# Attention scores: eight half-filled array tiles against four full ones with block-diagonal keys

## The chip, the cores and the metric

The kernel runs on one core of a Trainium2 chip. A core has TensorE (matrix products into PSUM), VectorE, ScalarE and GpSimd (elementwise work, named DVE, ACT and POOL in the profile), and SyncE (SP), whose queue issues most DMAs. The engines run their own instruction streams and meet at semaphores. The metric is the device time of one execution in microseconds; lower is better.

## The reference

The input x has 2048 rows of 512 values in bf16. Both branches read the same layer norm of it, and the output is x plus both branches.

```python
def _A_ref(x, wqkv, wo):
    H = 32; Dh = D // H; W = 256          # Dh = 16
    q, k, v = ...                          # of x @ wqkv, by heads
    scores = jnp.einsum("bhqd,bhkd->bhqk", q, k) * (Dh ** -0.5)
    mask = (idx[:, None] - idx[None, :] >= 0) & (idx[:, None] - idx[None, :] < W)
    p = _softmax(jnp.where(mask[None, None], scores, -1e9), axis=-1)
    o = jnp.einsum("bhqk,bhkd->bhqd", p, v)
    return (lambda x, *d: x.transpose(*d))(o, 0, 2, 1, 3).reshape(B, S, D) @ wo

def _B_ref(x, w_gate, w_up, w_down):       # F = 1792
    g = jnp.einsum("bsd,df->bsf", x, w_gate)
    u = jnp.einsum("bsd,df->bsf", x, w_up)
    return jnp.einsum("bsf,fd->bsd", g * u, w_down)

xn = _layernorm(x, axis=-1)
return x + _A_ref(xn, A_wqkv, A_wo) + _B_ref(xn, B_w_gate, B_w_up, B_w_down)
```

A has 32 heads of only 16 dimensions, and each query sees the 256 keys up to its own place.

## The kernel before

**Tiling.** The rows are cut into four chunks of 512 (T = 0 to 3). The 512 columns of Q and K are four groups (c = 0 to 3) of 128, which lie on the 128 partitions with the 512 rows of the chunk along the free dimension: `proj_qk` multiplies and copies one such tile from PSUM. Eight heads of 16 dimensions share a tile; every 32 partitions (a row group e of TensorE's array) hold an even head in the first 16 and an odd head in the last 16. Keys are taken in blocks of 64, queries in runs of 64 to 320.

**Scores.** `scores` makes one step: a batch of two or three pieces with 512 query columns in all. A piece is one block of 64 keys of one group c against a run of queries, for all eight heads. TensorE's array is used in tiles of 32 rows by 64 columns, so that eight small matmuls stand beside each other: four row groups e by two parities `par`. The even head (par 0) is multiplied with the plain K from the first 16 rows. The odd head (par 1) uses 32 rows of a second tile `Ko`, in which the even head's rows are zero. `Ko` is made by VectorE from `K` by a product with the per-partition scalar `odd` (0 or 1), at L262. The scores land in S, four PSUM banks of [128, 512], with the even head's 64 keys on partitions 0 to 63 and the odd head's on 64 to 127. S has one buffer. ScalarE then writes P = exp(S / 4) for all four banks at once (L319). GpSimd (`triangle`, L158) and VectorE (`mask_diag`, L343) zero what the window excludes.

**Values.** `values` (L366) multiplies P with V or VS (V with its halves swapped, by DMA), in 64x32 array tiles. There are two PSUM banks per (T, c), and mostly two groups are done in one burst, 192 matmuls. VectorE transposes the result (L372), and `divide` normalises it.

**The rest.** `proj_v`, `gate`, `up`, `down` and `wo` are plain 128x128 matmuls with 512 columns. All of them, and `proj_qk` and `values`, take their PSUM banks from one ring of four (`ps_m`).

**What sets the order.** The order on every engine is written out by a planner in `run`. There are 75 score steps (15 for T = 0, 20 for each later chunk). Between two steps, `fill` issues "fillers", mostly half a projection (two matmuls of 512 columns), until a target of TensorE time is reached; `SHIFT` moves this target at some steps. The planner counts in units of one such matmul. `book` keeps a count of when ScalarE and VectorE come free; `copy` gives each copy out of PSUM to the one that its booking says would be done first. The constants `EXP`, `MASK`, `HALF`, `COPY` and so on are the booked costs. They steer the choices and are no instructions themselves. In `first_chunk` the copies of K(0, 0) and K(0, 1) go to VectorE and that of Q(0, 0) to ScalarE; the first score step follows.

Of the kernel before, what the change touches and what calls it, by code (L numbers as in the profile page):

```python
# [7 lines left out]
BF16 = mybir.dt.bfloat16  # L8
F32 = mybir.dt.float32
# [16 lines left out]
GAP = 10.6  # L26
PAIRS = ((0,), (1,), (2,), (3,)), ((0, 1), (2, 3)), ((0, 1), (2, 3)), ((0, 1), (2,))
SHIFT = {20: -2, 21: -5, 22: -8, 23: -11, 24: -14, 26: -10, 27: -7, 28: -3, 62: 3, 63: 6, 64: 12, 66: 12, 67: 11, 68: 9, 69: 6, 70: 3}
MASKED, FIRST_DIVIDE, SECOND_DIVIDE = 8, 8, 24
COPY = dict(act=2.8, dve=3.2)  # L30
EXP, MASK, HALF, SUMS, DIVIDE, TURN, STATS = 8.7, 1.9, 1.7, 4.2, 8.2, 6.1, 4.2


class Kernel:
# [26 lines left out]
    def setup(self):  # L61
        nc, const, NT, NF = self.nc, self.const, self.NT, self.NF
        self.x = const.tile([128, NT, 512], BF16, name="x")
        self.Wqkv = const.tile([128, 4, 1536], BF16, name="Wqkv")
        self.Wo = const.tile([128, 4, 512], BF16, name="Wo")
        self.Wg = const.tile([128, 4, self.F], BF16, name="Wg")
        self.Wu = const.tile([128, 4, self.F], BF16, name="Wu")
        self.Wd = const.tile([128, NF, 512], BF16, name="Wd")
        xv = self.x_d.rearrange("(t p) d -> p t d", p=128)
        wq = self.w_d["qkv"].rearrange("(k p) n -> p k n", p=128)  # L70
        wg = self.w_d["g"].rearrange("(k p) n -> p k n", p=128)
        wu = self.w_d["u"].rearrange("(k p) n -> p k n", p=128)
        for lo, hi in ((0, 1), (1, 2), (2, 4)):
            nc.sync.dma_start(out=self.x[:, lo:hi, :], in_=xv[:, lo:hi, :])  # L74
        for lo in (1024, 512, 0):
            nc.sync.dma_start(out=self.Wqkv[:, :, lo:lo + 512], in_=wq[:, :, lo:lo + 512])
        h = self.F // 2
        for lo in (0, h):
            nc.sync.dma_start(out=self.Wg[:, :, lo:lo + h], in_=wg[:, :, lo:lo + h])
            nc.sync.dma_start(out=self.Wu[:, :, lo:lo + h], in_=wu[:, :, lo:lo + h])  # L80
            if lo == 0:
                nc.sync.dma_start(out=self.x[:, 4:8, :], in_=xv[:, 4:8, :])
        nc.sync.dma_start(out=self.Wd[:], in_=self.w_d["d"].rearrange("(f p) n -> p f n", p=128))
        wo = self.w_d["o"].rearrange("(c p) n -> p c n", p=128)
        for c in range(4):
            nc.sync.dma_start(out=self.Wo[:, c, :], in_=wo[:, c, :])
        for lo, hi in ((8, 10), (10, 12), (12, NT)):
            nc.sync.dma_start(out=self.x[:, lo:hi, :], in_=xv[:, lo:hi, :])

        warm = const.tile([128, 1], F32, name="warm")  # L90
        nc.vector.memset(warm[:], 0.0)
        nc.scalar.activation(out=warm[:], in_=warm[:], func=ACT.Exp)
        self.idle = const.tile([128, 128], BF16, name="idle")
        nc.vector.memset(self.idle[:], 0.0)
        self.keep_busy(40)
        ident = const.tile([128, 128], BF16, name="ident")
        nc.gpsimd.memset(ident[:], 0.0)
        nc.gpsimd.affine_select(out=ident[:], in_=ident[:], compare_op=ALU.not_equal, fill=1.0,
                                base=0, pattern=[[-1, 128]], channel_multiplier=1)
        self.ident = ident  # L100
        pi = const.tile([128, 1], I32, name="pi")
        nc.gpsimd.iota(pi[:], pattern=[[0, 1]], base=0, channel_multiplier=1)
        podd = const.tile([128, 1], I32, name="podd")
        nc.vector.tensor_scalar(out=podd[:], in0=pi[:], scalar1=4, scalar2=1,
                                op0=ALU.arith_shift_right, op1=ALU.bitwise_and)
        self.odd = const.tile([128, 1], F32, name="odd")
        nc.vector.tensor_copy(out=self.odd[:], in_=podd[:])
        self.mhalf = const.tile([128, 4], F32, name="mhalf")
        nc.gpsimd.memset(self.mhalf[:], -0.5)
        self.diag = const.tile([128, 64], BF16, name="diag")  # L110
        self.far = const.tile([128, 64], BF16, name="far")
        nc.gpsimd.memset(self.diag[:], BIG)
        nc.gpsimd.memset(self.far[:], BIG)
        for half in (slice(0, 64), slice(64, 128)):
            self.triangle(self.diag[half], True)
            self.triangle(self.far[half], False)
        self.xnT, self.Q, self.hT, self.OT = {}, {}, {}, {}
        self.K, self.Ko, self.V, self.VS = {}, {}, {}, {}
        self.strips, self.parts, self.at = {}, {}, {}
        self.stock = []  # L120
        self.new_values()
# [124 lines left out]
    def proj_qk(self, T, c, is_k, ks=range(4), engine=None):  # L246
        nc = self.nc
        lo = 512 * is_k + 128 * c
        ps = self.bank(ks, "qkp")
        for k in ks:  # L250
            nc.tensor.matmul(ps[:], lhsT=self.Wqkv[:, k, lo:lo + 128], rhs=self.xnT[T][:, :, k, :],  # L251
                             start=(k == 0), stop=(k == 3))
        if 3 not in ks:
            return
        if is_k:
            self.K[T, c] = self.kpool.tile([128, 512], BF16, tag="K", name="K")
            self.Ko[T, c] = self.kpool.tile([128, 512], BF16, tag="Ko", name="Ko")
        else:
            self.Q[T, c] = self.qpool.tile([128, 512], BF16, tag="Q", name="Q")
        self.copy((self.K if is_k else self.Q)[T, c][:], ps[:], engine)  # L260
        if is_k:
            nc.vector.tensor_scalar(out=self.Ko[T, c][:], in0=self.K[T, c][:],  # L262
                                    scalar1=self.odd[:, 0:1], scalar2=None, op0=ALU.mult)
            self.book("dve", HALF)

    def first_chunk(self):

# [32 lines left out]
    def scores(self, T, pieces):  # L300

        nc = self.nc
        S = self.s_tiles.tile([128, 4, 512], F32, tag="S", name="S")
        P = self.ppool.tile([128, 4, 512], BF16, tag="P", name="P")
        col = 0
        for c, m, q0, q1 in pieces:
            U, j = divmod(8 * T + m, 8)
            keys, q, n = slice(64 * j, 64 * j + 64), 64 * q0, 64 * (q1 - q0 + 1)
            for par in range(2):
                for e in range(4):  # L310
                    rows = slice(32 * e, 32 * e + 16 + 16 * par)
                    nc.tensor.matmul(S[64 * par:64 * par + 64, e, col:col + n],  # L312
                                     lhsT=(self.Ko if par else self.K)[U, c][rows, keys],
                                     rhs=self.Q[T, c][rows, q:q + n],
                                     start=True, stop=True, tile_position=(32 * e, 64 * par),
                                     skip_group_check=True)
            self.parts.setdefault((T, c), []).append((P, col, m, q, n))
            col += n
        nc.scalar.activation(out=P[:, :, 0:col], in_=S[:, :, 0:col], func=ACT.Exp, scale=0.25)  # L319
        self.book("act", EXP)  # L320
        self.masked = self.free["act"]
        self.strips[(T, pieces)] = P
        for at in self.places(pieces, 4):
            for half in (slice(0, 64), slice(64, 128)):
                self.triangle(P[half, :, at:at + 64], False)
# [199 lines left out]

    def run(self):
        self.xns, self.stats, self.sums = {}, {}, {}
        self.now, self.free = 0, dict(act=0, dve=0)
        self.setup()
        NCH = self.NCH  # L530
# [21 lines left out]
        def fill(upto, group):  # L552
            nonlocal spent, n
            while n < len(work):
                cost, f, before, after = work[n]
                if after is not None and after > valued:
                    break
                if spent + cost / 2 > upto and not any(
                        w[2] is not None and w[2] <= group for w in work[n:]):
                    break  # L560
                spent += cost
                self.now = spent
                f()
                n += 1
                while pending and spent >= pending[0][0]:
                    pending.pop(0)[1]()

# [5 lines left out]
        held = None  # L573
        for g, s in enumerate(steps):
            keys = due.get(g, [])
            if held is None:
                valued = ready
                fill(-1, g + len(keys) // 2)
# [87 lines left out]
```

The softmax here doesn't subtract the row's maximum and nothing guards it: scores larger than these inputs give would overflow.

## Time and profile before

| | before |
|---|---|
| median of 3 runs | 264.86 us (264.67 to 265.57) |
| profiled execution, its own time | 265.39 us |
| its span in the profile | 263.7 us |
| TensorE busy | 259.4 us (98%) |
| VectorE busy | 175.1 us (66%) |
| ScalarE busy | 175.5 us (67%) |
| GpSimd busy | 116.9 us (44%) |
| score matmuls (L312) | 1440 in 75 steps |
| `Ko` products (L262) | 16, mean 404 ns |
| granted TensorE clock | full over the whole span |

In the profile a line names a kernel line, an engine, an operation, and tiles as out<-in with their shapes; "x4" counts instructions, and the busy time and mean duration follow. A bracket such as [0.17 <-PE qkp L251] is the idle time before an instruction and what ended it. TensorE has two rows: PE for matmuls and PEld for the loads of their stationary operand. A list of waits has, on each line, who waited for whom, then the total in us, how many times, and the longest.

### The profile page before, as it was taken

To read this page: it belongs to the slowest core of one execution; us is meant where nothing else is said; L and a number is where in the kernel's file an instruction comes from. 1 tells how busy PE (TensorE), PEld (TensorE's weight loads), DVE (VectorE), ACT (ScalarE), POOL (GpSimd) and SP (SyncE) were. 2 spreads that over 40 slices of the span, in tenths; PEclk is the share of its full clock that TensorE was granted. 3 is DMA by queue.
4 is the path that set the end of the run, shared out by engine and by line. 5 is a ranking of instruction groups with operands and counts; after the bars stand their busy time and mean duration, and the time that the engine had idled before them with its cause. 6 is when DMAs were issued, how large, how long until landed. Compare 5 with 4: busy or idle time off the path is not lost.

```text
span 263.7 us, 8896 instructions
## 1 busy us (share of the span) xinstructions
PE 259.4 (98%) x3890; PEld 120.9 (46%) x3890; DVE 175.1 (66%) x342; ACT 175.5 (67%) x141; POOL 116.9 (44%) x278
## 2 busy tenths in 40 slices
PE   8999999999999999999999999999999999999996
PEld 8444444444444544444544454444544445444453
DVE  6677888877845497567873669766685135977344
ACT  3376788888856866677776566767777546787600
POOL 6216342425457645334456644544453451463600
PEclk9999999999999999999999999999999999999999
DMA  6999921220002600002001310000100100000002
GB/s 180 378 357 340 281 29 22 24 47 4 0 25 57 84 2 0 4 0 47 5 0 42 81 45 2 0 2 19 32 4 0 42 21 22 5 0 2 4 2 80
DMA packets 19431, 15.12 MB, mean 57 GB/s; under 512 B 7360, under 2 KB 19392, under 8 KB 19392
## 3 DMA queue, kind: packets, MB, share of 16 engines
q1 hardware_dynamic: 18848, 14.26, 19.9%
q8 instruction: 30, 0.49, 0.8%
q10 hardware_dynamic: 544, 0.30, 0.4%
q14 instruction: 9, 0.07, 0.1%
HBM read 9.70 MB, written 2.10 MB: 45 GB/s over the span
## 4 chain that ended last, share of the span: by engine, by line
PE 96%; DMA 2%; SPq 0%; issue 0%; DVE 0%
PE gp L395 19%; PE up L406 19%; PE psd L428 17%; PE qkp L251 11%; PE S L312 10%; PE acc L366 6%; PE vp L239 5%; PE psd L434 5%; PE L L428 2%; DMA Wqkv<-in_A_wqkv_dram 2%; PE L L434 1%; PE L L366 0%; SPq L74 0%; PE xTp L209 0%; DVE x L444 0%
## 5 line engine op out<-in xcount | busy, mean ns | idle before, releaser
L319 ACT ACTIVATE P<-S 128x2048 bf16<-128x2048 f32 x75 | 140.7, 1876 | 50.6 <-PE S L312 46.8
L158 POOL TENSOR_SCALAR_AFFINE_SELECT P<-P 64x256 bf16<-64x256 bf16 x224 | 100.9, 450 | 126.3 <-ACT P L319 112.1
L395 PE MATMUL gp<-xnT,Wg 128*128 128x512 bf16 x224 | 60.1, 380 | 0.0
L406 PE MATMUL up<-xnT,Wu 128*128 128x512 bf16 x224 | 59.1, 380 | 0.0
L411 DVE TENSOR_TENSOR hT<-up,gsb 128x512 bf16<-128x512 f32 x56 | 38.3, 685 | 19.3 <-PE up L406 13.7
L428 PE MATMUL psd<-Wd,hT 128*128 128x512 bf16 (+1 forms) x210 | 48.0, 369 | 0.0
L343 DVE TENSOR_TENSOR P<-P,diag 128x512 bf16<-128x512 bf16 (+1 forms) x75 | 29.4, 392 | 6.1 <-ACT P L319 6.1
L428 PEld LDWEIGHTS <-hT 128*128 128x128 bf16 x238 | 21.3, 98 | 25.1 <-issue 2.9
L406 PEld LDWEIGHTS <-Wu 128*128 128x128 bf16 x224 | 20.5, 98 | 25.4 <-issue 2.5
L395 PEld LDWEIGHTS <-Wg 128*128 128x128 bf16 x224 | 20.3, 98 | 25.1 <-issue 1.9
L312 PE MATMUL S<-Q,K 16*64 16x320 bf16 (+4 forms) x720 | 31.0, 260 | 0.0
L312 PE MATMUL S<-Q,Ko 32*64 32x320 bf16 (+4 forms) x720 | 30.9, 260 | 0.0
L251 PE MATMUL qkp<-xnT,Wqkv 128*128 128x512 bf16 x128 | 29.9, 380 | 0.0
L230 ACT ACTIVATE gsb<-gp 128x512 bf16<-128x512 f32 x39 | 22.9, 596 | 8.2 <-PE gp L395 7.4
L312 PEld LDWEIGHTS <-K 16*64 16x64 bf16 x720 | 12.1, 103 | 30.7 <-issue 30.7
L372 DVE STREAM_TRANSPOSE at<-acc 128x512 f32<-128x512 f32 x30 | 19.1, 688 | 8.9 <-PE acc L366 8.9
L444 DVE TENSOR_TENSOR x<-psd,x 128x512 bf16<-128x512 f32 (+1 forms) x15 | 9.7, 655 | 15.7 <-PE psd L434 15.7
L251 PEld LDWEIGHTS <-Wqkv 128*128 128x128 bf16 x128 | 11.7, 98 | 14.5 <-issue 1.6
L366 PE MATMUL acc<-P,VS 64*32 64x320 bf16 (+4 forms) x672 | 17.7, 253 | 0.0
L366 PE MATMUL acc<-P,V 64*32 64x320 bf16 (+4 forms) x672 | 17.5, 253 | 0.0
L366 PEld LDWEIGHTS <-V 64*32 64x32 bf16 x720 | 15.1, 91 | 2.2 <-issue 1.6
L239 PE MATMUL vp<-Wqkv,xnT 128*128 128x512 bf16 x64 | 15.3, 380 | 0.5 <-DMA Wqkv<-in_A_wqkv_dram 0.5
(54 smaller groups left out, 200.2 us busy)
## 6 DMA issues: line engine op xcount, KB each, us to landing
out_dram<-x SPq DMA_DIRECT2D x15, 128.0 KB, 1.7
Wg<-in_B_w_gate_dram SPq DMA_DIRECT2D x2, 896.0 KB, 11.4
Wu<-in_B_w_up_dram SPq DMA_DIRECT2D x2, 896.0 KB, 13.7
Wd<-in_B_w_down_dram SPq DMA_DIRECT2D x1, 1792.0 KB, 17.2
Wqkv<-in_A_wqkv_dram SPq DMA_DIRECT2D x3, 512.0 KB, 5.9
x<-in_A_x_dram SPq DMA_DIRECT2D x2, 512.0 KB, 8.7
VS<-V SPq DMA_DIRECT2D x6, 144.0 KB, 2.6
x<-in_A_x_dram SPq DMA_DIRECT2D x3, 256.0 KB, 6.6
```

Of the source, the lines that this page charges most:

```text
L158: nc.gpsimd.affine_select(out=v, in_=v, pattern=pattern + [[1 if diag else -1, 64]], compare_op=ALU.is_ge if diag else ALU.is_gt, fill=0.0 ...
L230: nc.scalar.activation(out=out, in_=in_, func=ACT.Copy)
L239: nc.tensor.matmul(ps[:], lhsT=self.xnT[T][:, b, k, :], rhs=self.Wqkv[:, k, 1024:1536], start=(k == 0), stop=(k == 3))
L251: nc.tensor.matmul(ps[:], lhsT=self.Wqkv[:, k, lo:lo + 128], rhs=self.xnT[T][:, :, k, :], start=(k == 0), stop=(k == 3))
L312: nc.tensor.matmul(S[64 * par:64 * par + 64, e, col:col + n], lhsT=(self.Ko if par else self.K)[U, c][rows, keys], rhs=self.Q[T, c][rows, ...
L319: nc.scalar.activation(out=P[:, :, 0:col], in_=S[:, :, 0:col], func=ACT.Exp, scale=0.25)
L343: self.nc.vector.tensor_tensor(out=v, in0=v, op=ALU.min, in1=self.diag.unsqueeze(1).unsqueeze(1).to_broadcast([128, 4, n, 64]))
L366: nc.tensor.matmul(accs[par][32 * e:32 * e + 32, q:q + n], lhsT=v, rhs=P[rows, e, col:col + n], start=(i == 0), stop=(i == len(todo) - 1), ...
L395: nc.tensor.matmul(ps[:], lhsT=self.Wg[:, k, 128 * f:128 * f + 128], rhs=self.xnT[T][:, :, k, :], start=(k == 0), stop=(k == 3))
L406: nc.tensor.matmul(ps[:], lhsT=self.Wu[:, k, 128 * f:128 * f + 128], rhs=self.xnT[T][:, :, k, :], start=(k == 0), stop=(k == 3))
L411: nc.vector.tensor_tensor(out=self.hT[T, f][:], in0=ps[:], in1=self.gsb[:], op=ALU.mult)
L428: nc.tensor.matmul(ps, lhsT=self.hT[T, f][:, 128 * b:128 * b + 128], rhs=self.Wd[:, f, c0:c1], start=(f == 0), stop=False)
```

## The change

One K tile of twice the width takes the place of the pair K and Ko. In it, each block of 64 keys stands twice: once with the odd head's rows zeroed (64 columns for the even head), once with the even head's rows zeroed. It is the stationary operand of one matmul of 32 rows by 128 columns per row group, so that a piece has four matmuls instead of eight, with the same queries and the same places in S. The plain K is copied out of PSUM into a work tile `k` (two buffers). VectorE makes the wide tile from it by one TENSOR_TENSOR product with `pair`, a [128, 2] tile of zeros and ones that is read with step 0 along the keys. The planner books this product at BOTH = 2.9 units instead of HALF = 1.7. Besides, 260 no-ops are put into TensorE's stream, up to three behind each filler: 110 from step 27 on and 150 from step 57 on.

```diff
+PADS = {27: 110, 57: 150}
...
-EXP, MASK, HALF, SUMS, DIVIDE, TURN, STATS = 8.7, 1.9, 1.7, 4.2, 8.2, 6.1, 4.2
+EXP, MASK, BOTH, SUMS, DIVIDE, TURN, STATS = 8.7, 1.9, 2.9, 4.2, 8.2, 6.1, 4.2
...
-        self.odd = const.tile([128, 1], F32, name="odd")
-        nc.vector.tensor_copy(out=self.odd[:], in_=podd[:])
+        self.pair = const.tile([128, 2], BF16, name="pair")
+        nc.vector.tensor_copy(out=self.pair[:, 1:2], in_=podd[:])
+        nc.vector.tensor_scalar(out=self.pair[:, 0:1], in0=self.pair[:, 1:2], scalar1=-1.0, scalar2=1.0,
+                                op0=ALU.mult, op1=ALU.add)
...
         if is_k:
-            self.K[T, c] = self.kpool.tile([128, 512], BF16, tag="K", name="K")
-            self.Ko[T, c] = self.kpool.tile([128, 512], BF16, tag="Ko", name="Ko")
+            self.K[T, c] = self.kpool.tile([128, 1024], BF16, tag="K", name="K")
+            k = self.work.tile([128, 512], BF16, tag="k", name="k")
+            self.copy(k[:], ps[:], engine)
+            nc.vector.tensor_tensor(out=self.K[T, c].rearrange("p (j r n) -> p j r n", r=2, n=64), op=ALU.mult,
+                                    in0=k.rearrange("p (j n) -> p j n", n=64).unsqueeze(2).to_broadcast([128, 8, 2, 64]),
+                                    in1=self.pair.unsqueeze(1).unsqueeze(3).to_broadcast([128, 8, 2, 64]))
+            self.book("dve", BOTH)
         else:
             self.Q[T, c] = self.qpool.tile([128, 512], BF16, tag="Q", name="Q")
-        self.copy((self.K if is_k else self.Q)[T, c][:], ps[:], engine)
-        if is_k:
-            nc.vector.tensor_scalar(out=self.Ko[T, c][:], in0=self.K[T, c][:],
-                                    scalar1=self.odd[:, 0:1], scalar2=None, op0=ALU.mult)
-            self.book("dve", HALF)
+            self.copy(self.Q[T, c][:], ps[:], engine)
...
-            keys, q, n = slice(64 * j, 64 * j + 64), 64 * q0, 64 * (q1 - q0 + 1)
-            for par in range(2):
-                for e in range(4):
-                    rows = slice(32 * e, 32 * e + 16 + 16 * par)
-                    nc.tensor.matmul(S[64 * par:64 * par + 64, e, col:col + n],
-                                     lhsT=(self.Ko if par else self.K)[U, c][rows, keys],
-                                     rhs=self.Q[T, c][rows, q:q + n],
-                                     start=True, stop=True, tile_position=(32 * e, 64 * par),
-                                     skip_group_check=True)
+            keys, q, n = slice(128 * j, 128 * j + 128), 64 * q0, 64 * (q1 - q0 + 1)
+            for e in range(4):
+                rows = slice(32 * e, 32 * e + 32)
+                nc.tensor.matmul(S[:, e, col:col + n], lhsT=self.K[U, c][rows, keys],
+                                 rhs=self.Q[T, c][rows, q:q + n],
+                                 start=True, stop=True, tile_position=(32 * e, 0),
+                                 skip_group_check=True)
...
                 n += 1
+                for _ in range(min(3, self.pads)):
+                    self.nc.tensor.nop("pad", nofuse=True)
+                    self.pads -= 1
...
             keys = due.get(g, [])
+            self.pads += PADS.get(g, 0)
```

More of the change, by code (lines that the diff above doesn't have):

```diff
@@ L117, in setup @@
         self.xnT, self.Q, self.hT, self.OT = {}, {}, {}, {}
-        self.K, self.Ko, self.V, self.VS = {}, {}, {}, {}
+        self.K, self.V, self.VS = {}, {}, {}
         self.strips, self.parts, self.at = {}, {}, {}
@@ L527, in run @@
         self.xns, self.stats, self.sums = {}, {}, {}
+        self.pads = 0
         self.now, self.free = 0, dict(act=0, dve=0)
```

## The prediction

> **What bounds the kernel now.** I read the page first (busy shares and the chain that ended last), then TensorE's list of waits, then the timeline of single score steps, then VectorE's timeline where K is made.
>
> ```profile
> span 263.7 us, 8896 instructions
> PE 259.4 (98%) x3890; PEld 120.9 (46%) x3890; DVE 175.1 (66%) x342; ACT 175.5 (67%) x141; POOL 116.9 (44%) x278
> ...
> PE 96%; DMA 2%; SPq 0%; issue 0%; DVE 0%
> ```
>
> ```profile
> PE wps L127 <- DVE idle L94: 1.1, 1, 1.1
> PE vp L239 <- DMA Wqkv<-in_A_wqkv_dram: 0.5, 1, 0.5
> ```
>
> TensorE is busy 98% of the span and is 96% of the chain. A busy row alone proves little for pipelined matmuls, so the second fence matters: these two waits, both before 8 us, are all that TensorE's matmuls ever wait for. From there the span is a plain sum of matmul starts: a 512-column matmul takes a slot of 216 ns (4 in 0.86 us), whatever VectorE and ScalarE do. So an edit counts if it shortens TensorE's own sequence, or if it delays another engine so far that TensorE begins to wait. The sequence around one score step:
>
> ```profile
> 66.20 0.59 PE L395 MATMUL gp<-xnT,Wg 128*128 128x512 bf16 x2
> 66.73 0.25 PE L312 MATMUL S<-Q,K 16*64 16x128 bf16 x4
> 66.74 0.25 PE L312 MATMUL S<-Q,Ko 32*64 32x128 bf16 x4
> 66.81 0.20 PE L312 MATMUL S<-Q,K 16*64 16x64 bf16 x4
> 66.82 0.20 PE L312 MATMUL S<-Q,Ko 32*64 32x64 bf16 x4
> 66.83 0.31 PE L312 MATMUL S<-Q,K 16*64 16x320 bf16 x4
> 66.85 0.31 PE L312 MATMUL S<-Q,Ko 32*64 32x320 bf16 x4
> 67.09 0.39 PE L395 MATMUL gp<-xnT,Wg 128*128 128x512 bf16 x1
> ```
>
> The eight matmuls of a piece run side by side: all start within 23 ns, and a piece costs about its own columns once, not eight times. At full resolution the starts are 3.3 ns apart (66.727, 66.730, ... 66.750). The next piece starts 3.3 ns after the eighth has streamed its 128 columns (66.750 + 0.053 + 0.003 = 66.807); a third piece follows its predecessor per tile, 1 to 7 ns beyond its columns. Before the group lie 96 ns and behind it 93 ns in which nothing streams. In all 75 steps the group itself is 263 to 268 ns for 512 columns (213 ns): about 50 ns are the stagger of eight.
>
> [...] 91 to 97 ns at each of the changes that I looked at, 128x128 to 32x64 and back, and to and from 64x32 alike, so I take the same for 32x128. [...] The page shows 30 such packets on q8 (0.49 MB), and TensorE's 2 x 3890 records are 30.4 blocks, so q8 is TensorE's stream.
>
> **The change, part by part.**
>
> *Score matmuls, 1440 to 720.* The columns streamed per piece stay. With four starts instead of eight, the stagger at the first changeover falls from 26.6 to 13.3 ns and that at the end from 23.3 to 10: 26.6 ns per step, 75 steps, **-2.0 us**, all on the chain. The mode changes stay: 0. Bounds: [...] with 64 columns visible as 27 ns (a load that starts at 66.809 is followed by its matmul at 66.835), 128 would take 53; that adds about 26 ns in the 28 places where a 64-column piece precedes another: +0.7 us. I take 0.
>
> *K.* Before: copy out of PSUM, then a product of 352 to 552 ns (L262). After: the same copy into a work tile (two buffers, freed by a product that follows at once) and a TENSOR_TENSOR of 1024 elements. [...] it extends the mask's row (L343: 381 ns for 512, 550 for 768) to about 0.65 us. [...] it extends `on<-at,rz` (691 ns for 512[...]) to 1.22 us. So +0.3 or +0.87 us for each of 16. [...] Against it stands the diff's own price: a planner unit is 0.21 us (EXP 8.7 for 1.876, COPY 3.2 for 0.69, MASK 1.9 for 0.39, HALF 1.7 for 0.352), so BOTH = 2.9 is 0.61 us, and the other constants all match their rows. I take **0.65**, narrowly, and keep 1.22 as the main rival. The tight places are two. First, the first score step:
>
> ```profile
> 12.41 0.69 DVE L232 CAST K<-qkp 128x512 bf16<-128x512 f32 x1 [0.17 <-PE qkp L251]
> 13.14 0.35 DVE L262 TENSOR_SCALAR Ko<-K,odd 128x512 bf16<-128x512 bf16 x1
> ```
>
> The scores start at 14.03; at 0.65 K is ready at 13.79, so nothing waits. Every other K stands ready 3.5 to 46 us early. Second, where chunk 1's K falls into a stretch in which VectorE has no pause (56.2 to 61.7 us):
>
> ```profile
> 59.70 0.68 DVE L232 CAST K<-qkp 128x512 bf16<-128x512 f32 x1
> 60.42 1.01 DVE L262 TENSOR_SCALAR Ko<-K,odd 128x512 bf16<-128x512 bf16 x2
> 61.35 0.40 DVE L343 TENSOR_TENSOR P<-P,diag 128x512 bf16<-128x512 bf16 x1
> 61.68 0.68 DVE L232 CAST Q<-qkp 128x512 bf16<-128x512 f32 x1
> 62.40 0.69 DVE L232 CAST K<-qkp 128x512 bf16<-128x512 f32 x1
> ```
>
> Behind the products queue a mask and two copies, whose PSUM banks the values of 64.37 need: the copies end at 62.36 and 63.09, so there are 2.0 and 1.3 us to spare. Three products at +0.3 push them by 0.9 at most: no wait.
>
> *Booking and setup.* BOTH books 1.2 units (0.26 us) more, which can turn a copy from VectorE to ScalarE where the two are nearly level; ScalarE has 46.8 us of waiting before its exponentials, so 0. The extra 128x1 operation for `pair` (154 ns, row of L104) lies before VectorE's first statistics, which wait for the load of x: 0. No DMA, no queue of SP or POOL is touched.
>
> *No-ops.* 260 on TensorE, 3 behind a filler, so 87 groups. A filler of two 512-column matmuls lasts 432 ns and is 4 instructions, and q8's refills show the stream being read some 30 to 100 instructions ahead of execution. [...] If each drained the array, the nearest row is the 94 ns of a mode change. What they do move is where the 256-instruction blocks fall. The five bursts of 384 value instructions (2.2 us each) begin, counting TensorE's records, at places 8, 8, 232, 208, 208 of a block. With the score instructions gone and the no-ops in, it is about 24, 198, 230, 14, 228; without the no-ops the fourth would begin at about 160, where the fetch of the next block would be asked for at the burst's start and needed 1.8 us later, against roughly 2.0 us that a fetch takes (0.9 to its packet, 1.0 to 1.4 in it). Cost 0 with them; up to 0.4 us a burst where I miscount.
>
> *Sum:* -2.0 us. The profiled execution took 265.39 us (span 263.7, 1.7 around it), 0.5 above the median; so 263.4 for such an execution and **262.9 us** for a median.
>
> **The rivals.**
>
> *A[...].* [...] Then K of the first step is ready at 14.38 + 0.06, and TensorE waits 0.4. In chunk 1 the delay of 0.87 from the product at 55.51 is never recovered; with two more, the Q copy ends near 64.9 and the K copy near 65.65, so the values of 64.37 wait up to 1.3 us for a bank. Later chunks have pauses of 0.7 us between copies and lose 0 to 0.25. Net -2.0 + 0.4 + 1.3 = -0.3: **264.6**.
>
> *B, slower: the no-ops are not hidden.* If TensorE's sequencer handles one only when the array is empty, each of 87 groups behind a filler, at places between steps 27 and 33 and 57 and 65, costs a drain of 94 ns or more: +8.2 - 2.0, **271**. It decides from 23 ns a group (2.0 / 87). Against it: nothing in the no-op waits for a semaphore, and the stream is read well ahead.
>
> *C, the four tiles are not cheaper.* If starts are spaced by the columns loaded, not by instructions, [...] the gain shrinks to between 0 and 1.3: **263.6 to 264.9**. Against it: 64x32 groups load half the columns and show the same stagger.
>
> **How the numbers follow.** A difference of 0.3% (0.8 us) is about what a measurement of this kernel can tell from none. Forecast 0.47, A 0.33, C 0.08, B or a fetch wait of its size 0.12. The forecast and its near variants fall under 264.1; A straddles the border (a quarter faster, half same, a quarter slower); C is shared. That gives faster 0.57, same 0.25, slower 0.18. The range 262.1 to 265.8 holds the forecast with a slightly larger gain[...], A with 0.9 us more of waiting, and C; it leaves out B.
>
> **What would show it.** TensorE still without waits after 8 us; score groups of about 237 ns; mode changes of 91 to 97 ns; the product's row at 0.65 us; q8 with 26 packets. A product near 1.22 us, with TensorE waiting at 14 and 64 us, is A. A longer slot for fillers after steps 27 and 57 is B. The forecast is wrong if the group stays at 263 ns.

## The result and the profile after

The changed kernel takes 264.84 us (median of 6 runs), the kernel before 264.84 us in the same comparison: a ratio of 0.9996, 95% interval 0.9983 to 1.0009. The forecast of 262.9 us was wrong. What the profile shows is its rival A, 264.6 us, in which the product takes about 1.22 us.

The page of the kernel after, in its heads, its chain and three of its groups (mean ns of one behind the busy time):

```profile
span 263.1 us, 7719 instructions
...
PE 257.9 (98%) x3170; PEld 118.5 (45%) x3170; DVE 187.9 (71%) x341; ACT 176.7 (67%) x143; POOL 123.8 (47%) x278
...
PE 94%; DVE 4%; issue 1%; ACT 0%
...
L315 PE MATMUL S<-Q,K 32*128 32x320 bf16 (+4 forms) x720 | 29.9, 254 | 0.3 <-DVE K L262 0.3
...
L315 PEld LDWEIGHTS <-K 32*128 32x128 bf16 x720 | 10.3, 92 | 31.1 <-issue 30.3
...
L262 DVE TENSOR_TENSOR K<-k,pair 128x1024 bf16<-128x1024 bf16 x16 | 20.1, 1262 | 2.0 <-ACT k L233 1.7
```

The number of score matmuls is halved, as the diff says. A score step got shorter with it. The one whose lines the prediction shows is now:

```profile
66.97 0.59 PE L397 MATMUL gp<-xnT,Wg 128*128 128x512 bf16 x2
67.50 0.40 PE L315 MATMUL S<-Q,K 32*128 32x128 bf16 x12
67.83 0.39 PE L397 MATMUL gp<-xnT,Wg 128*128 128x512 bf16 x1
```

From its first matmul to the next filler 0.33 us pass, where it was 0.36 (66.73 to 67.09). But VectorE now has a share in the chain that ended last, 4%, where it had 0%, and its busy time grew by 12.8 us. The product's row says why: 1262 ns, not 650. TensorE's list of waits shows what it did:

```profile
PE wps L130 <- DVE idle L95: 1.1, 1, 1.1
PE acc L368 <- DVE Q L235: 0.6, 1, 0.6
PE acc L368 <- DVE k L235: 0.4, 1, 0.4
PE S L315 <- DVE K L262: 0.3, 1, 0.3
```

The first line is the start-up wait of before. The other three are new, and all name VectorE. The list counts idle time after the modelled end of the matmul before. Counted from start to start, beyond the columns and the usual gap, the three pauses are 659, 531 and 388 ns: 1.58 us.

Where they come from is seen in VectorE's timeline of chunk 1 (start, duration, instruction):

```profile
60.09 0.68 DVE L235 CAST k<-qkp 128x512 bf16<-128x512 f32 x1
60.80 2.57 DVE L262 TENSOR_TENSOR K<-k,pair 128x1024 bf16<-128x1024 bf16 x2
63.29 0.62 DVE L345 TENSOR_TENSOR P<-P,diag 128x512 bf16<-128x512 bf16 x1
63.83 0.68 DVE L235 CAST Q<-qkp 128x512 bf16<-128x512 f32 x1
64.43 0.68 DVE L235 CAST k<-qkp 128x512 bf16<-128x512 f32 x1
```

Two products in a row take 2.57 us. Behind them come a mask and two copies, which end at 64.51 and 65.11 us. These copies empty the two PSUM banks into which the next values go, and TensorE's timeline shows the values stopping twice, once for each bank:

```profile
63.57 0.40 PE L315 MATMUL S<-Q,K 32*128 32x192 bf16 x8
64.56 0.24 PE L368 MATMUL acc<-P,V 64*32 64x128 bf16 x4 [0.60 <-DVE Q L235]
65.16 0.24 PE L368 MATMUL acc<-P,VS 64*32 64x128 bf16 x4 [0.36 <-DVE k L235]
65.17 0.29 PE L368 MATMUL acc<-P,V 64*32 64x256 bf16 x4
```

**The account.** From the first `qkp` matmul to the start of the last matmul TensorE took 249.47 us before and 249.20 after, 0.27 us less. The 75 score groups exceed their columns (0.417 ns each, from slots of 216 ns for 512 columns and 56 for 128) by 1.77 us in all, before by 3.83: -2.06. Entering the 32x128 mode takes 98.7 ns, entering 32x64 took 95.7: +0.2 over 75 steps. The three pauses: +1.58. The sum is -0.28. (The spans of 263.7 and 263.1 differ by more, since the kernel before was profiled with a pause of 0.67 us at 6.5 us, for the load of Wqkv.) The account is one of two profiled executions. The medians do not differ at all, and their interval, -0.45 to +0.24 us, has room for -0.28.

### The profile page after: what moved, and what is told of

Read it like the earlier page. It is cut to its first block, busy times and chain, and to the rows that moved or that the text cites. A ratio compares the mean times of both kernels' runs of the same rounds, so it can differ in the third digit from the quotient of the medians.

```text
span 263.1 us, 7719 instructions
## 1 busy us (share of the span) xinstructions
PE 257.9 (98%) x3170; PEld 118.5 (45%) x3170; DVE 187.9 (71%) x341; ACT 176.7 (67%) x143; POOL 123.8 (47%) x278
## 4 chain that ended last, share of the span: by engine, by line
PE 94%; DVE 4%; issue 1%; ACT 0%
PE up L408 19%; PE gp L397 19%; PE psd L430 17%; PE S L315 9%; PE qkp L254 8%; PE acc L368 6%; PE vp L242 5%; PE psd L436 5%; PE L L430 2%; PE wps L130 2%; DVE K L262 1%; DVE k L235 1%; PE L L436 1%; DVE P L345 1%; PE L L368 0%
## 5 line engine op out<-in xcount | busy, mean ns | idle before, releaser
L161 POOL TENSOR_SCALAR_AFFINE_SELECT P<-P 64x256 bf16<-64x256 bf16 x224 | 107.2, 479 | 117.7 <-ACT P L321 99.1
L345 DVE TENSOR_TENSOR P<-P,diag 128x512 bf16<-128x512 bf16 (+1 forms) x75 | 30.9, 412 | 5.9 <-ACT P L321 5.9
L315 PE MATMUL S<-Q,K 32*128 32x320 bf16 (+4 forms) x720 | 29.9, 254 | 0.3 <-DVE K L262 0.3
L315 PEld LDWEIGHTS <-K 32*128 32x128 bf16 x720 | 10.3, 92 | 31.1 <-issue 30.3
L262 DVE TENSOR_TENSOR K<-k,pair 128x1024 bf16<-128x1024 bf16 x16 | 20.1, 1262 | 2.0 <-ACT k L233 1.7
```

The lines of the kernel that those rows point to most:

```text
L161: nc.gpsimd.affine_select(out=v, in_=v, pattern=pattern + [[1 if diag else -1, 64]], compare_op=ALU.is_ge if diag else ALU.is_gt, fill=0.0 ...
L315: nc.tensor.matmul(S[:, e, col:col + n], lhsT=self.K[U, c][rows, keys], rhs=self.Q[T, c][rows, q:q + n], start=True, stop=True, tile_posit ...
L345: self.nc.vector.tensor_tensor(out=v, in0=v, op=ALU.min, in1=self.diag.unsqueeze(1).unsqueeze(1).to_broadcast([128, 4, n, 64]))
```

## The experiments

The first four ran together, and so did the last four. Each is compared with the kernel before on its own chip (264.80 and 264.83 us).

| kernel | score matmuls of a piece | product | no-ops | us | ratio to before (95%) |
|---|---|---|---|---|---|
| after | 4 | slow | 110 + 150 | 264.84 | 0.9996 (0.9983 to 1.0009) |
| e1, wide pair | 4 | fast | 110 + 150 | 263.30 | 0.9942 (0.9930 to 0.9953) |
| e2, no no-ops | 4 | slow | none | 271.41 | 1.0231 (1.0205 to 1.0257) |
| e3, before with no-ops | 8 | as before | 110 + 150 | 270.16 | 1.0210 (1.0185 to 1.0236) |
| e4, eight tiles | 8 | slow | 110 + 150 | 271.72 | 1.0270 (1.0242 to 1.0298) |
| e5, eight tiles | 8 | slow | none | 266.60 | 1.0070 (1.0057 to 1.0082) |
| e6, before, one block of no-ops | 8 | as before | 256 from step 0 | 265.02 | 1.0011 (1.0002 to 1.0021) |
| e7, true price booked | 4 | slow | 110 + 150 | 263.94 | 0.9963 (0.9951 to 0.9975) |
| e8, other places | 4 | fast | 192 + 150 | 269.94 | 1.0186 (1.0161 to 1.0212) |

**e1: the product's second operand with a step of one.** My theory was that the product's rate alone costs the gain; the rival, that the gain goes elsewhere. `pair` is stored with each of its values 64 times, so that the second operand has a step of one.

```diff
-        self.pair = const.tile([128, 2], BF16, name="pair")
-        nc.vector.tensor_copy(out=self.pair[:, 1:2], in_=podd[:])
+        self.pair = const.tile([128, 2, 64], BF16, name="pair")
+        nc.vector.tensor_copy(out=self.pair[:, 1, :], in_=podd[:].to_broadcast([128, 64]))
...
-                                    in1=self.pair.unsqueeze(1).unsqueeze(3).to_broadcast([128, 8, 2, 64]))
+                                    in1=self.pair.unsqueeze(1).to_broadcast([128, 8, 2, 64]))
```

> The change with pair stored as a full [128, 2, 64] tile, so that the product's second operand has step 1; nothing else differs. Theory [...]: the product falls from 1262 ns to about 0.65 us, TensorE waits for nothing after 9 us, 264.84 - 1.58 = 263.3 us, ratio 0.994 to before. Rival (the gain goes elsewhere: no-ops, fetches, other array mode): product faster, time within 0.3 us of 264.8.

Measured: 263.30 us. The product's row, and TensorE's whole list of waits:

```profile
L262 DVE TENSOR_TENSOR K<-k,pair 128x1024 bf16<-128x1024 bf16 x16 | 11.4, 717 | 3.2 <-ACT k L233 2.8
```

```profile
PE wps L130 <- DVE idle L95: 1.1, 1, 1.1
PE vp L242 <- DMA Wqkv<-in_A_wqkv_dram: 0.5, 1, 0.5
```

The elements, the instructions and the order are the same; only the step of one operand differs. The product falls by 545 ns, all three pauses go, and 1.54 us come back where 1.58 were expected (the medians of two comparisons; between the profiled executions it is 1.64 us, from the first `qkp` to the last matmul). This run beats both kernels and is the version to keep.

**e2: without the no-ops.**

```diff
-PADS = {27: 110, 57: 150}
+PADS = {}
```

> The change without its 260 no-ops. Theory (no-ops only move the instruction blocks): nothing changes up to step 27; the burst at 187.6 us would then begin near place 160 of a block and its next block be fetched late, a pause of 0 to 0.4 us inside that burst; elsewhere the same: 264.8 to 265.2 us. Rival (the no-ops cost TensorE time): 264.8 less up to 1 us. Rival (they do nothing at all): 264.84.

Measured: 271.41 us. No theory had this size: without its 260 no-ops the change is 2.3% slower than before. Each value matmul is two instructions, a load and the matmul, so that a burst of 192 matmuls is 384 instructions. TensorE's timeline inside the second of the five bursts of this size:

```profile
126.82 0.40 PE L368 MATMUL acc<-P,VS 64*32 64x320 bf16 x7
128.63 0.28 PE L368 MATMUL acc<-P,VS 64*32 64x256 bf16 x1 [1.42 <-issue]
128.63 0.39 PE L368 MATMUL acc<-P,V 64*32 64x256 bf16 x8
```

The line of seven merges four matmuls of 320 columns with three of the next four, of 256 columns. The fourth of these starts 1.69 us after the third, and "issue" says that no semaphore is behind it. Burst two, three and four each have one such pause: 1.58, 1.90 and 1.65 us beyond the columns. In all three the last instruction ahead of it stands at place 192 of a block of 256, counted from 0 over all of TensorE's recorded instructions. I read this place as the border of an instruction block. The packets of q8, which the page calls "instruction", fit that: each has 16 KiB, and before has 30 of them for 30 such places in 7780 recorded instructions, the change 26 for 26 in 6600, no-ops included. A burst of 384 that holds two borders would then need a second new block 1.5 us after the first; that this block is not there is my reading. In e2, between the two borders q8 starts a single packet, 0.6 to 0.8 us after the first border is executed; the packet takes 1.0 to 1.2 us, and TensorE goes on 3.2 to 3.5 us after that border. Between the packet's end and that moment lie 1.3 to 1.5 us that no record explains, so what a fetch consists of stays open. A second cost follows from the first. Three stretches around the pause of burst three (bounds and length, then each engine's busy us and count, then the granted clock):

```profile
core 0: us, PE busy (x) PEld busy (x) DVE busy (x) ACT busy (x) POOL busy (x), PEclk, DMA share, GB/s
155.00:162.00 7.00, 5.28 (x218) 3.22 (x216) 3.10 (x6) 3.80 (x3) 2.65 (x7) 1.00 0.10 27
162.40:165.90 3.50, 3.50 (x11) 1.24 (x9) 2.96 (x7) 2.29 (x2) 0.82 (x2) 0.52 0.02 5
166.00:170.00 4.00, 4.00 (x41) 1.59 (x38) 3.44 (x7) 2.33 (x2) 0.63 (x2) 1.00 0.00 0
```

For 3.5 us behind the pause the granted clock is 0.52 and each 512-column matmul takes 211 ns more: 1.68 us. Three pauses (5.12) and this make 6.8 us. From the first `qkp` to the last matmul the run is 6.9 us longer than the change. The fall of the clock does not come every time: of the six executions two have the full mean clock and took 269.7 and 269.8 us, about the pauses alone; three with 0.992 to 0.994 took 271.5 to 272.2; one took 271.4 with the full clock on record, and its excess is not explained.

**e3: the kernel before, with the no-ops.** If the no-ops cost time themselves, they should cost it here too.

```diff
+PADS = {27: 110, 57: 150}
...
+                for _ in range(min(3, self.pads)):
+                    self.nc.tensor.nop("pad", nofuse=True)
+                    self.pads -= 1
...
+            self.pads += PADS.get(g, 0)
```

> The kernel before with the same 260 no-ops, nothing else. Theory (hidden behind fillers, and no burst gets a bad place: about 8, 118, 86, 62, 212): 264.84, ratio 1.000. Rival (each group of no-ops drains the array, 94 ns x 87): 273 us.

Measured: 270.16 us, a miss. It is not the rival's mechanism either: the fillers around the no-ops keep their slots. Again bursts two to four pause, by 2.11, 1.73 and 1.80 us, each time at place 192. The granted clock by fortieths of the span shows one fall behind a pause:

```profile
PEclk9999999999999999999799999999999999999999
```

That execution took 272.33 us. The five others kept the full clock and took 269.7 to 270.5, so the median holds the pauses and not the fall. What cures the change spoils the kernel before, since its bursts stand elsewhere.

**e4: the change with eight tiles.** It was meant to separate the gain of four tiles from the loss of the product. The wide K is read by the eight 32x64 matmuls of before, half by half.

```diff
...
-                nc.tensor.matmul(S[:, e, col:col + n], lhsT=self.K[U, c][rows, keys],
...
+            for par in range(2):
+                for e in range(4):
...
+                    nc.tensor.matmul(S[64 * par:64 * par + 64, e, col:col + n],
+                                     lhsT=self.K[U, c][rows, 128 * j + 64 * par:128 * j + 64 * par + 64],
...
```

> The change with its wide K, its slow product, booking and no-ops, but with the eight 32x64 matmuls of the kernel before, which read the two halves of the wide K. Theory (gain of the four tiles 2.06 - 0.21 us, loss of the waits about 1.6 us, independent of each other): score groups of 264 ns again, waits of TensorE at 14 and 64 us as in the change: 264.84 + 1.85 = 266.7 us, ratio 1.007. Rival (the four tiles bring nothing and the product costs nothing): 264.8.

Measured: 271.72 us, a miss by 5 us. The trace has the waits at 14 and 64 us as expected (384, 628 and 532 ns), and beside them pauses of 2.12, 1.89 and 1.54 us at place 192: with eight tiles and 260 no-ops the bursts stand as in e3. The comparison was spoilt by the places, so it was repeated as e5.

**e5: e4 without the no-ops.** Its bursts stand where they do in the kernel before.

```diff
-PADS = {27: 110, 57: 150}
+PADS = {}
```

> The wide K, its slow product and booking, the eight 32x64 matmuls of before, and no no-ops, so that every burst of values stands at the same place of an instruction block as in the kernel before. Theory (the product's waits and the gain of four tiles are separate terms; the excess of the run with eight tiles and no-ops was block fetches): no pause inside bursts, waits at 14 and 64 us of about 1.55 us in all: 266.4 us, ratio 1.006. Rival (eight tiles with the wide K lose by themselves): about 271.7 us again.

Measured: 266.60 us. The waits are 382, 627 and 531 ns, 1.54 us, and no burst pauses. So the product costs the same with four tiles and with eight, and four tiles bring 266.60 - 264.84 = 1.8 us (1.86 between the profiled executions), as 2.06 - 0.2 says.

**e6: one whole block of no-ops.** Nearly the same number of no-ops as in e3, but placed so that every large burst stands where it stood.

```diff
+PADS = {0: 256}
...
```

The lines that place them are those of e3.

> The kernel before with 256 no-ops from step 0 on, three behind a filler: as many as in the change, but a whole block, so that every burst of 384 instructions stands where it stood. Theory (what costs is the place of the bursts in the blocks, not the no-ops): 264.84 us, ratio 1.000. Rival (the no-ops themselves cost, some 5 us for 256): 270 us.

Measured: 265.02 us, ratio 1.0011 (1.0002 to 1.0021). The interval leaves them 0.6 us at most, 0.2 by the medians; in e3, 260 of them "cost" 5.4. It is the places that count.

**e7: the product's true price in the planner.**

```diff
-EXP, MASK, BOTH, SUMS, DIVIDE, TURN, STATS = 8.7, 1.9, 2.9, 4.2, 8.2, 6.1, 4.2
+EXP, MASK, BOTH, SUMS, DIVIDE, TURN, STATS = 8.7, 1.9, 5.7, 4.2, 8.2, 6.1, 4.2
```

> The change with BOTH = 5.7 units, the measured 1.26 us, instead of 2.9; the product stays slow. By the planner's arithmetic the copy of Q(1, 2) then goes to ScalarE. Theory (the waits at 64 us are VectorE's queue): the first of the two waits there goes and the second copy comes 0.68 us earlier, so TensorE waits about 0.6 us there instead of 1.19; 0.39 at 14 us stays: 264.84 - 0.55 = 264.3 us. Rival (ScalarE's exponential is late instead): 264.8 us or more.

Measured: 263.94 us. VectorE's timeline in chunk 1 no longer has the copy of Q between the mask and the copy of k:

```profile
60.63 2.57 DVE L262 TENSOR_TENSOR K<-k,pair 128x1024 bf16<-128x1024 bf16 x2
63.12 0.62 DVE L345 TENSOR_TENSOR P<-P,diag 128x512 bf16<-128x512 bf16 x1
63.66 0.68 DVE L235 CAST k<-qkp 128x512 bf16<-128x512 f32 x1
```

TensorE waits once there, 656 ns in place of 659 + 531. That accounts for 0.53 us of the 0.9 us between the medians of this kernel and of the change, which were timed in different comparisons. The two profiled executions differ by 0.88 us: 0.58 from the first `qkp` to the last matmul, 0.16 ahead of it and 0.14 behind it. The last two were not traced to a cause. The reading of the queue holds: take one copy out of it and one wait goes.

**e8: a rule for the places.** From e2 to e4 I read that a burst pauses if it holds two borders, that is, if it starts at places 64 to 192. This is e1 with other no-ops.

```diff
-PADS = {27: 110, 57: 150}
+PADS = {27: 192, 57: 150}
```

> The full pair tile (fast product) with 192 no-ops from step 27 on instead of 110. Rule from the runs so far: a burst of 384 instructions pauses if it holds two block boundaries, that is if it starts at places 64 to 192 of a block, counted from TensorE's first recorded instruction; boundaries at 192. The bursts would then start near 27, 3 to 27, 59, 99, 57. Expected: the fourth burst alone pauses, 1.5 to 2.1 us, at its second boundary; the third, at 59, does not: 263.3 + 1.8 = 265.1 us, up to 266.8 if the TensorE clock falls behind it. Rival (boundaries elsewhere): another burst pauses, or none (263.3).

Measured: 269.94 us. Bursts three, four and five pause (1.60, 1.96, 1.51 us), not the fourth alone: a miss by 4.8 us. The pauses are 5.07 of the 6.6 us by which this run is longer than e1; behind the fourth burst's pause the granted clock falls once more. TensorE's timeline at the end of the third:

```profile
156.25 0.29 PE L368 MATMUL acc<-P,VS 64*32 64x256 bf16 x4
156.48 0.26 PE L315 MATMUL S<-Q,K 32*128 32x192 bf16 x3
158.17 0.39 PE L315 MATMUL S<-Q,K 32*128 32x192 bf16 x5 [1.43 <-issue]
```

The border falls in the score step that follows the burst at once. The burst of the rule must therefore include the next score step (16 to 24 instructions), and bursts at 57 and 59 have their second border there. The traces of e3 and e4 had shown this before the run: the last pause of each stands in front of a score matmul. With this the rule fits every burst of 384 in these ten kernels: the 12 with two borders pause, the 38 with one do not. But the amended rule was read from the runs and was not tested by another.

## Why the prediction was wrong

- **TensorE is a plain sum: right.** In the change it waits at three places, in e1 at none behind 9 us, and the sum of its starts gives each time.
- **-2.0 us from the score groups: right.** Measured -2.06; the group takes 235 to 239 ns, 237 was foretold. The mode changes were taken at 0 and cost 0.2 us in all, since the entry takes 98.7 ns. The longer loads of the prediction's bound did not come: 128-column loads at L315 take 92 ns, where the 64-column loads at L312 took 103.
- **The product at 0.65 us: this step failed.** I had two prices, both my estimates from other rows; no row of before has a bf16 second operand with step 0 inside. Extended from `on<-at,rz` (691 ns for 512 elements) it came to 1.22 us; with the growth of `x<-psd,x` in the same trace (292 ns for 128 elements, 681 for 512) it is 1.21. Extended from the mask's row it came to 0.65. I took the second because the planner's BOTH is near it (0.61) and its neighbours match their rows. The product ran in 1262 ns, and e1 makes it 717 by the step alone. The 0.65 was too low even for that: the mask's own two figures, 381 ns for 512 elements and 550 for 768, go on in a straight line to 719 for 1024. A booked cost is an intention of the program, not a measurement.
- **What followed from the price was worked out rightly, as rival A.** First step: 0.4 foretold, 0.39 measured. Chunk 1: up to 1.3 foretold, 1.19 measured. Later chunks: 0 to 0.25 foretold, 0 measured. A gave -0.3 us; the account of the profiled executions gives -0.28.
- **The no-ops at 0, an estimate: right within 0.2 us** (e6), and so was what they are for (e2). The 8.2 us of rival B did not occur.
- **The fetches: right in kind, mis-sized.** I put at most 0.4 us on a burst, and expected it in one only, if the no-ops were left out. It was three bursts of 1.6 to 1.9 us, and 1.7 us of lower clock behind one (e2). Two terms failed: I took the first recorded instruction as the border of a block, while the pauses put the borders at place 192; and I took 2.0 us for a fetch, while 3.2 to 3.5 pass in e2 from the first executed border to the instruction behind the second. With the first term goes the lead of 30 to 100 instructions: paired in order with the places 192, the 30 packets of before start between 31 instructions ahead of theirs and 171 behind it. In the change itself these errors cost nothing, as each of its five bursts holds one border. That was in part luck: with the border in the wrong place, the sum could not tell a good place from a bad one.

## What to carry to other kernels

When two prices for a new operation disagree and neither was measured on the operation's own access pattern, time that pattern first (1262 ns here, where 650 was taken); and where a broadcast leaves the innermost step of a 16-bit operand at zero, a constant tile that spells the values out can nearly halve the instruction (1262 to 717 ns here). A saving on the bounding engine counts only if the engine that pays for it still empties the banks in time (1.58 us of pauses took back most of 2.06 here), so look for the stretch in which that engine has no pause. When an edit changes the number of TensorE instructions, list the dense bursts and their places in the 256-instruction blocks before and after: between e1 and e8 a move by 82 no-ops cost 6.6 us, where the edit brings 1.5.

## What the runs showed of the hardware beyond this

- A dense run on TensorE, here 384 instructions in 2.2 us and a score step behind it, stopped for 1.5 to 2.1 us in all 12 cases in which two places 192 of the 256-instruction blocks fell into it (e2, e3, e4, e8). 256 such instructions last 1.4 to 1.7 us, and TensorE went on 3.1 to 3.7 us after the first of the two places. That a late instruction block is the reason is read from the places and from the packets of q8.
- Behind one pause in each trace of e2, e3 and e8 (1.90, 2.11 and 1.96 us) the granted clock fell. In e2 it is 0.52 over 3.5 us, and the 1.68 us that this adds nearly double the pause. Behind e4's pause of 2.12 us it did not fall; what decides this stays open.
- The no-ops of a group of three follow each other mostly 70 to 71 ns apart, at times 90 ns or more. Three of them all but disappear behind a filler of 432 ns: 256 cost 0.2 us by the medians (e6).
